# Reordering the first microseconds of a GeGLU feed-forward kernel: x's first rows by token halves, gate rows first on ScalarE's queue

## The chip, the cores and the metric

The kernel runs on one core of one Trainium2 chip. The metric is the device time of one execution in microseconds (us). The kernel before took 272.92, 274.2 and 273.94 us in three runs, so its median is 273.94 us and the runs are 1.28 us (0.47%) apart from end to end. One more execution was profiled; every line of a profile shown here comes from such a profiled execution, and its times count from the first instruction of the span.

Engine names in the profile: PE is TensorE's matmul, PEld TensorE's weight load, DVE is VectorE, ACT is ScalarE, POOL is GpSimd, SP is SyncE. SPq and ACTq are the instruction streams of SP and ACT when they issue DMAs (transfers).

## The reference

```python
B, S, D, F = 32, 32, 1024, 3584          # x is 1024 tokens by 1024, all bf16
def reference(x, w_gate, w_up, w_down):
    return (gelu_tanh(x @ w_gate) * (x @ w_up)) @ w_down
```

Two products of 1024 x 1024 by 1024 x 3584, an elementwise GELU and product, and one product back of 1024 x 3584 by 3584 x 1024.

## The kernel before

**Tiling.** Both stages are done on quadrants, by a scheme that needs seven products of half-sized quadrants in place of eight (Strassen's, in the form with few additions). The 1024 tokens are two blocks of `NB` = 512, the inner dimension D is two halves of 512. A half is `KD` = 4 slices of 128 (128 is `P`, the number of partitions). In the code `b11`, `b12`, `b21`, `b22` are the four quadrants of x transposed (inner dimension on partitions, tokens along the row): first index the half of D, second index the token block. `b21`, the one that matters here, is the second half of D for the first 512 tokens, as four slices `k` of 128 x 512. The gate weight's quadrants are called a11 and a12 (first and second half of D), the up weight's a21 and a22.

**The first stage** walks the 28 feature tiles of 128 columns in 14 chunks of two. For the first `NAHEAD` = 24 tiles one of the products, a12 times `b21`, is done before everything else, in six groups of `KB` = 4 tiles (`a12_ahead[0]` to `a12_ahead[5]`, each 128 x 4 x 512 of `w_gate`), and parked in SBUF in the tiles `ahead`. This is what PE does in the first 26 us or so, and the change lies wholly in how that work starts. The second stage (lines 407 to 590) is the product with `w_down`; the change does not touch it.

**How b21 comes in.** x lies in memory with tokens as rows, and PE wants the inner dimension on partitions. Slices 2 and 3 of `b21`, and the other three quadrants, come by transposing DMAs (`load_xT`, line 216). For slices 0 and 1 (`KQ` = 2) that is done on PE: `load_nat` (line 196) brings x's rows as they are into `x_nat`, PE transposes them in pieces of 128 x 128 against an identity matrix (line 264), and VectorE copies the result from the PSUM tile `tp` into `b21` (line 267). One call `transposed(dt)` does one slice: two halves of 256 tokens, two pieces each, a copy after each half.

**Order of work.** The whole kernel is under a manual schedule: each engine executes its instructions in the order in which the code issues them, and an instruction that waits holds everything behind it on its engine. Nothing is reordered by a planner. So the order around the change is:

- SP's queue: `x_nat` for slice 0 (all 512 tokens, 128 KB), then slices 0 and 1 of `a12_ahead[0]` one by one (128 KB each), the transposing DMA for slices 2 and 3 of `b21`, and then the rest of `a12_ahead`, the first weights and the other quadrants of x.
- ScalarE's queue: `probe`, a read of a few bytes of `w_gate` into a tile that nothing reads; `x_nat` for slice 1 (128 KB); slices 0 and 1 of `a12_ahead[1]` (256 KB); then its compute instructions, of which the first is a GELU that loads the function table.
- PE: `NWARM` = 6 matmuls of ones into `warm_ps`, whose result nobody reads; the four transposes of slice 0; then the loop of lines 327 to 332. It goes over slice `k` and token half, with four half products (128 x 256, one for each tile `j` of `a12_ahead[0]`) in each of its four rounds. After the first round come the four transposes of slice 1. Then eight products with `a12_ahead[1]` (slices 0 and 1), and so on through the groups.
- VectorE: the four copies out of `tp`, then its half of the copies to `ahead`.

What PE waits for here: the first transpose for `x_nat`; a half product for its slice of `a12_ahead[0]` and for VectorE's copy of its half of `b21`.

Of the kernel before, what the change touches and what calls it, by code (L numbers as in the profile page):

```python
# [13 lines left out]
def kernel(  # L14
# [20 lines left out]
    nc = tc.nc  # L35
    P = nc.NUM_PARTITIONS
    fp32 = mybir.dt.float32
    f32r = mybir.dt.float32r
    bf16 = mybir.dt.bfloat16
# [10 lines left out]
    KD = DT // 2  # L50
# [4 lines left out]
    KQ = DT // 4  # L55
    HF = FT // 2
    MT = NB // P
    NWARM = 6
    KB = 4
    QF = HF // 2  # L60
    batches = [(0, KB), (KB, QF), (QF, QF + KB), (QF + KB, HF)]
# [2 lines left out]
    wg_r = w_gate.rearrange("(dt dp) f -> dp dt f", dp=P)  # L64
# [8 lines left out]
    xpool = one.enter_context(tc.tile_pool(name="x", bufs=1))  # L73
# [33 lines left out]
    def acc(tag):  # L107
        return ps1.tile([P, NB], fp32, name=f"ps{tag}", tag=tag, bufs=BANKS[tag])
# [5 lines left out]
    b21 = xpool.tile([P, KD, NB], bf16, name="b21")  # L114
# [72 lines left out]
    ones_w = nc.const_aps.tensor(1.0, [P, P], bf16)  # L187
    ones_m = nc.const_aps.tensor(1.0, [P, NB], bf16)
    ident = xpool.tile([P, P], bf16, name="ident")
    make_identity(nc, ident)  # L190
    NB_P = NB // P
    HALF = NB_P // 2
    x_nat = spool.tile([P, NB_P, KQ * P], bf16, name="x_nat", tag="s1")

    with tc.manual_schedule():
        def load_nat(eng, dt, p0, p1):
            eng.dma_start(  # L197
                out=x_nat[:, p0:p1, dt * P : (dt + 1) * P],
                in_=xf[p0 * P : p1 * P, (KD + dt) * P : (KD + dt + 1) * P].rearrange("(b p) d -> p b d", p=P),
            )  # L200

        assert KQ == 2
        load_nat(nc.sync, 0, 0, NB_P)


        probe = xpool.tile([P // 8, KQ, 2], bf16, name="probe")
        nc.scalar.dma_start(out=probe, in_=wg_r[::8, KD : KD + KQ, :2])

        def load_ahead(i, k0, k1, eng=nc.sync):
            f0 = i * KB  # L210
            eng.dma_start(
                out=a12_ahead[i][:, k0:k1, :],
                in_=wg_r[:, KD + k0 : KD + k1, f0 * P : (f0 + KB) * P],
            )

        def load_xT(nb, d0, d1):
            t = ((b11, b12), (b21, b22))[d0 // KD][nb]
            nc.sync.dma_start_transpose(
                out=t[:, d0 % KD : (d1 - 1) % KD + 1, :], in_=xf[nb * NB : (nb + 1) * NB, d0 * P : d1 * P]
            )  # L220

        load_ahead(0, 0, 1)
        load_nat(nc.scalar, 1, 0, NB_P)
        load_ahead(0, 1, 2)
        load_xT(0, KD + KQ, DT)
        load_ahead(1, 0, KQ, nc.scalar)
        a12_ahead += [spool.tile([P, KD, KB * P], bf16, name="a12b", tag=t) for t in ("s2", "s4", "s1", "s3")]
        for i in (0, 1):
            load_ahead(i, KQ, KD)
# [24 lines left out]
        warm_ps = acc("A")  # L254
        for _ in range(NWARM):
            nc.tensor.matmul(warm_ps, lhsT=ones_w, rhs=ones_m, start=True, stop=True)

        tps = [[ps1.tile([P, HALF * P], bf16, name="tp", tag="A", bufs=BANKS["A"]) for _ in range(2)] for _ in range(KQ)]

        def transposed(dt):  # L260
            for half, tp in enumerate(tps[dt]):
                p0 = half * HALF
                for b in range(HALF):
                    nc.tensor.transpose(  # L264
                        tp[:, b * P : (b + 1) * P], x_nat[:, p0 + b, dt * P : (dt + 1) * P], ident
                    )
                nc.vector.tensor_copy(b21[:, dt, p0 * P : (p0 + HALF) * P], tp)

        transposed(0)

        def prod(ps, lhs, rhs, start):
            for k in range(KD):
# [9 lines left out]
        def product_ahead(ps, i, j, k0=0, k1=KD, cols=slice(None)):  # L282
            for k in range(k0, k1):
                nc.tensor.matmul(  # L284
                    ps[:, cols],
                    lhsT=a12_ahead[i][:, k, j * P : (j + 1) * P],
                    rhs=b21[:, k, cols],
                    start=(k == 0 and not cols.start),
                    stop=(k == KD - 1),
                    skip_group_check=True,  # L290
                )
# [35 lines left out]
        for k in range(KQ):  # L327
            for half in range(2):
                for j in range(KB):
                    product_ahead(ps[0][j], 0, j, k, k + 1, slice(half * HALF * P, (half + 1) * HALF * P))  # L330
                if k == half == 0:
                    transposed(1)
        for j in range(KB):
            product_ahead(ps[1][j], 1, j, 0, KQ)
        for i in (0, 1):
# [283 lines left out]
```

## Time and profile before

| | |
|---|---|
| three runs | 272.92, 274.2, 273.94 us |
| span of the profiled execution | 272.0 us |
| time of that execution around its span | not shown; the three runs are 0.9 to 2.2 us above the span |
| PE busy in the span | 267.1 us (98%) |
| VectorE, POOL, ScalarE busy | 74%, 44%, 43% |
| PE's first matmul | 0.78 us |
| first transpose | 3.30 us |
| first half product | 4.31 us |
| first matmul with slice 1 of `a12_ahead[0]` | 6.28 us |

The page's first parts give busy times and a row of 40 slices; its chain of waits names what the end of the span hangs on. Times of single instructions come from the timeline, which merges neighbours of one kind: a line gives the start, the length of the merged piece, the instruction and, in brackets, how long the engine stood idle before it and what released it. A matmul's length there includes the time until its result is out, so successive matmuls overlap; their pace is read from the distance of their starts.

### The profile page before, as it was taken

To read this page: it belongs to the slowest core of one execution; us is meant where nothing else is said; L and a number is where in the kernel's file an instruction comes from. 1 tells how busy PE (TensorE), PEld (TensorE's weight loads), DVE (VectorE), ACT (ScalarE), POOL (GpSimd) and SP (SyncE) were. 2 spreads that over 40 slices of the span, in tenths; PEclk is the share of its full clock that TensorE was granted. 3 is DMA by queue.
4 is the path that set the end of the run, shared out by engine and by line. 5 is a ranking of instruction groups with operands and counts; after the bars stand their busy time and mean duration, and the time that the engine had idled before them with its cause. 6 is when DMAs were issued, how large, how long until landed. Compare 5 with 4: busy or idle time off the path is not lost.

```text
span 272.0 us, 3399 instructions
## 1 busy us (share of the span) xinstructions
PE 267.1 (98%) x1199; PEld 193.4 (71%) x1212; DVE 201.2 (74%) x205; ACT 116.1 (43%) x189; POOL 119.3 (44%) x60
## 2 busy tenths in 40 slices
PE   8999999999999999999999999999999999999995
PEld 4444776886787688688688687764458888888884
DVE  1448998886976876876787458569999999997721
ACT  2335865545644643645636535434000307770000
POOL 1090099976995994994995978000000000000000
PEclk9999999999999999999999999999999999999999
DMA  7999130504505505415234290005981437855111
GB/s 174 323 227 281 39 99 17 158 25 130 154 2 154 154 4 154 128 27 157 69 88 118 50 319 17 0 2 182 356 273 60 158 112 253 276 187 174 54 61 58
DMA packets 56048, 35.86 MB, mean 132 GB/s; under 512 B 9824, under 2 KB 56032, under 8 KB 56032
## 3 DMA queue, kind: packets, MB, share of 16 engines
q1 hardware_dynamic: 52736, 33.17, 42.6%
q10 hardware_dynamic: 3296, 2.49, 2.9%
q8 instruction: 9, 0.15, 0.2%
q14 instruction: 7, 0.06, 0.1%
HBM read 31.72 MB, written 2.10 MB: 124 GB/s over the span
## 4 chain that ended last, share of the span: by engine, by line
PE 97%; DMA 1%; issue 0%; SPq 0%; DVE 0%
PE psA L273 38%; PE psA L425 24%; PE psC L273 19%; PE psC L425 7%; PE psA L284 5%; PE psC L284 3%; PE psC L588 1%; DMA a12a<-in_w_gate_dram 1%; SPq L197 0%; PE tp L264 0%; DVE o_last L589 0%
## 5 line engine op out<-in xcount | busy, mean ns | idle before, releaser
L273 PE MATMUL psA<-t,s 128*128 128x512 f32 x224 | 57.2, 397 | 0.0
L248 ACT ACTIVATE h<-c 128x512 bf16<-128x512 f32 x56 | 34.6, 631 | 41.6 <-DVE c L303 41.6
L273 PEld LDWEIGHTS psA<-t,s 128*128 128x128 f32 x224 | 42.1, 188 | 9.5
L170 POOL TENSOR_TENSOR s<-wu 128x1024 fp32r<-128x1024 bf16 x13 | 28.8, 2215 | 32.9 <-DMA wu<-in_w_up_dram 27.9
L171 POOL TENSOR_TENSOR s<-s,wg 128x1024 fp32r<-128x1024 f32 x14 | 31.7, 2263 | 15.0 <-DVE s L170 14.0
L173 POOL TENSOR_TENSOR s<-wg,wu 128x1024 fp32r<-128x1024 bf16 x13 | 28.4, 2188 | 0.0
L273 PE MATMUL psA<-b,wg 128*128 128x512 bf16 x119 | 27.8, 379 | 0.6
L273 PE MATMUL psA<-t,a22r 128*128 128x512 f32 x112 | 27.9, 391 | 0.0
L273 PE MATMUL psC<-t,s 128*128 128x512 f32 x112 | 27.9, 391 | 0.0
L273 PE MATMUL psC<-b22r,s 128*128 128x512 f32 x112 | 27.6, 389 | 0.0
L303 DVE TENSOR_TENSOR c<-sn,psA 128x512 f32<-128x512 f32 x32 | 21.8, 682 | 6.7 <-PE psA L273 5.7
L308 ACT COPY sn<-psC 128x512 f32<-128x512 f32 x28 | 16.4, 590 | 20.9 <-PE psC L273 15.2
L273 PEld LDWEIGHTS psC<-t,s 128*128 128x128 f32 x112 | 21.0, 188 | 4.5
L273 PEld LDWEIGHTS psA<-t,a22r 128*128 128x128 f32 x112 | 21.0, 188 | 4.5
L273 PEld LDWEIGHTS psC<-b22r,s 128*128 128x128 f32 x112 | 21.0, 188 | 4.4
L303 DVE TENSOR_TENSOR c<-sn,psC 128x512 f32<-128x512 f32 x28 | 19.2, 688 | 6.5 <-PE psC L273 6.5
L273 PEld LDWEIGHTS <-wg 128*128 128x128 bf16 x128 | 11.8, 98 | 15.3 <-issue 2.4
L172 POOL TENSOR_TENSOR s<-wg,s 128x1024 fp32r<-128x1024 bf16 x10 | 21.6, 2158 | 0.8
L402 DVE TENSOR_TENSOR lo<-c,h 128x512 bf16<-128x512 f32 x14 | 20.4, 1459 | 0.9
L308 ACT COPY sn<-psA 128x512 f32<-128x512 f32 x32 | 18.4, 592 | 6.1 <-PE psA L273 6.0
L303 DVE TENSOR_TENSOR c<-ahead,psA 128x512 f32<-128x512 f32 x24 | 16.4, 687 | 4.0 <-PE psA L273 2.4
L321 DVE TENSOR_TENSOR hi<-h,psA 128x512 bf16<-128x512 bf16 x14 | 9.6, 688 | 12.4 <-PE psA L273 12.4
(85 smaller groups left out, 381.0 us busy)
## 6 DMA issues: line engine op xcount, KB each, us to landing
wu<-in_w_up_dram SPq DMA_DIRECT2D x14, 512.0 KB, 4.0
wdb<-in_w_down_dram SPq DMA_DIRECT2D x12, 512.0 KB, 4.9
wg<-in_w_gate_dram SPq DMA_DIRECT2D x9, 512.0 KB, 5.2
wdb<-in_w_down_dram SPq DMA_DIRECT2D x12, 384.0 KB, 4.5
v<-in_w_down_dram SPq DMA_DIRECT2D x4, 512.0 KB, 6.4
out_dram<-o_sb ACTq DMA_DIRECT2D x15, 128.0 KB, 1.7
wg<-in_w_gate_dram SPq DMA_DIRECT2D x6, 256.0 KB, 4.6
v<-in_w_down_dram SPq DMA_DIRECT2D x4, 384.0 KB, 7.5
```

The lines of the kernel that those rows point to most:

```text
L170: yield engs[0].tensor_tensor(s1, a21, a22, ADD)
L171: yield engs[1].tensor_tensor(s2, s1, a11, SUB)
L172: yield engs[2].tensor_tensor(s4, a12, s2, SUB)
L173: yield engs[3].tensor_tensor(s3, a11, a21, SUB)
L248: nc.scalar.activation(h, src, ACT.Gelu_apprx_tanh)
L273: nc.tensor.matmul(ps, lhsT=lhs[:, k, :], rhs=rhs[:, k, :], start=(start and k == 0), stop=(k == KD - 1), skip_group_check=True,)
L284: nc.tensor.matmul(ps[:, cols], lhsT=a12_ahead[i][:, k, j * P : (j + 1) * P], rhs=b21[:, k, cols], start=(k == 0 and not cols.start), stop ...
L303: tt(t, s, ps, ADD)
L308: nc.scalar.copy(t, ps)
L321: tt(g_of(ft)[:, :NB], h0, psa, MUL)
L402: tt(g_of(ft)[:, NB:], added(sn5[fl], psa[fl]), h1[fl], MUL)
L425: nc.tensor.matmul(banks[m], lhsT=lhs(k)[:, m * P : (m + 1) * P], rhs=rhs(k), start=(start and k == 0), stop=(k == HF - 1), skip_group_che ...
```

## The change

It has four pieces, all in the head of the program.

1. `x_nat` for slice 0 comes in two transfers of 256 tokens (64 KB each), and slice 1 (128 KB) third, all three on SP's queue.
2. The `probe` read is gone. ScalarE's queue now begins with the two slices of `a12_ahead[0]` (128 KB each), followed by the 256 KB of `a12_ahead[1]` as before. SP's queue has lost the two slices of `a12_ahead[0]`, and its transposing DMA is the fourth transfer as it was before.
3. PE's warm-up is five matmuls of 128x512 in place of six. `transposed` now does one half of one slice. Only slice 0's first half (two transposes, one copy) stands ahead of the loop, followed by `NFILL` = 6 matmuls of 128x128 of ones into `warm_ps`.
4. After the first round of four half products come the other six transposes in a row: slice 0's second half, slice 1's first, slice 1's second; and VectorE's three copies after them.

Everything behind the loop is as before; PE's instructions are the old ones less one warm-up matmul, and six fillers more.

```diff
-    NWARM = 6
+    NWARM = 5
+    NFILL = 6
...
-        load_nat(nc.sync, 0, 0, NB_P)
-
-
-        probe = xpool.tile([P // 8, KQ, 2], bf16, name="probe")
-        nc.scalar.dma_start(out=probe, in_=wg_r[::8, KD : KD + KQ, :2])
+        load_nat(nc.sync, 0, 0, HALF)
+        load_nat(nc.sync, 0, HALF, NB_P)
+        load_nat(nc.sync, 1, 0, NB_P)
...
-        load_ahead(0, 0, 1)
-        load_nat(nc.scalar, 1, 0, NB_P)
-        load_ahead(0, 1, 2)
+        for k in range(KQ):
+            load_ahead(0, k, k + 1, nc.scalar)
+        load_ahead(1, 0, KQ, nc.scalar)
         load_xT(0, KD + KQ, DT)
-        load_ahead(1, 0, KQ, nc.scalar)
...
-        def transposed(dt):
-            for half, tp in enumerate(tps[dt]):
-                p0 = half * HALF
-                for b in range(HALF):
-                    nc.tensor.transpose(
-                        tp[:, b * P : (b + 1) * P], x_nat[:, p0 + b, dt * P : (dt + 1) * P], ident
-                    )
-                nc.vector.tensor_copy(b21[:, dt, p0 * P : (p0 + HALF) * P], tp)
-
-        transposed(0)
+        def transposed(dt, half):
+            p0, tp = half * HALF, tps[dt][half]
+            for b in range(HALF):
+                nc.tensor.transpose(tp[:, b * P : (b + 1) * P], x_nat[:, p0 + b, dt * P : (dt + 1) * P], ident)
+            nc.vector.tensor_copy(b21[:, dt, p0 * P : (p0 + HALF) * P], tp)
+
+        transposed(0, 0)
+        for _ in range(NFILL):
+            nc.tensor.matmul(warm_ps[:, :P], lhsT=ones_w, rhs=ones_w, start=True, stop=True)
...
                 if k == half == 0:
-                    transposed(1)
+                    for dt, h in ((0, 1), (1, 0), (1, 1)):
+                        transposed(dt, h)
```

## The prediction

> **What bounds the kernel now.** I read the page's busy times and chain first, to see whether a few tenths won in the head reach the end.
>
> ```profile
> PE 267.1 (98%) x1199; PEld 193.4 (71%) x1212; DVE 201.2 (74%) x205; ACT 116.1 (43%) x189; POOL 119.3 (44%) x60
> ...
> PE 97%; DMA 1%; issue 0%; SPq 0%; DVE 0%
> ```
>
> PE is busy for 98% of the span and the chain that ended last is 97% PE. So behind the head the kernel is one row of matmuls, and what the head gains or loses arrives at the end in full, unless PE then meets a transfer. The chain of the first 8 us, in order of time (start, length, what), shows what is not PE:
>
> ```profile
> 0.74 0.45 SPq L197
> 1.19 0.06 issue
> 1.25 3.02 DMA a12a<-in_w_gate_dram
> 4.26 0.05 issue
> 4.31 0.61 PE psC L284 x2
> ```
>
> SP issues `x_nat`, then the first gate slice; that lands at 4.27, and from 4.31 the chain is PE. The timeline of the head shows what PE did meanwhile:
>
> ```profile
> 0.78 2.72 PE L256 MATMUL psA<-const-bfloat16-1.0 128*128 128x512 bf16 x6 [0.78 <-PEq L603]
> 3.30 0.62 PE L264 MATMUL tp<-ident,x_nat 128*128 128x128 bf16 x4
> 3.75 0.51 DVE L267 COPY b<-tp 128x256 bf16<-128x256 bf16 x2 [3.75 <-PE tp L264]
> 4.31 0.61 PE L284 MATMUL psC<-b,a12a 128*128 128x256 bf16 x2 [0.39 <-DMA a12a<-in_w_gate_dram]
> 5.14 0.63 PE L264 MATMUL tp<-ident,x_nat 128*128 128x128 bf16 x4
> 5.57 0.53 PE L284 MATMUL psC<-b,a12a 128*128 128x256 bf16 x2
> 5.93 0.38 PE L284 MATMUL psA<-b,a12a 128*128 128x256 bf16 x2
> 6.28 1.64 PEld L284 LDWEIGHTS <-a12a 128*128 128x128 bf16 x13 [0.25 <-DMA a12a<-in_w_gate_dram]
> ```
>
> Paces, from distances of starts: up to 5.6 us a transpose costs 0.107 us (four from 5.14 to 5.57) and a 128x256 half product 0.21 (four from 4.31 to 5.14); from 5.93 a half product costs 0.11. The warm-up matmuls stand 0.43 apart, later 128x512 ones 0.216. So PE runs at half pace until about 5.85 us, although the page's clock row shows 9 throughout. Idle on PE: 0.39 us for the first gate slice, and about 0.13 before 6.28 for the second. Landings and the sharing of the DMA engines (bytes per issue, us to landing; then the two queues' share of the engines' time from 3.3 to 3.6 us, q1 being SP's and q10 ScalarE's):
>
> ```profile
> x_nat<-in_x_dram SPq DMA_DIRECT2D x1, 128.0 KB, 2.5
> x_nat<-in_x_dram ACTq DMA_DIRECT2D x1, 128.0 KB, 3.2
> a12a<-in_w_gate_dram SPq DMA_DIRECT2D x2, 128.0 KB, 3.7
> ...
> q1 hardware_dynamic: 59, 0.05, 49.2%
> q10 hardware_dynamic: 114, 0.03, 49.1%
> ```
>
> ```profile
> 2.20:2.70 0.50, 0.50 (x3) 0.15 (x1) 0.00 (x0) 0.41 (x1) 0.00 (x0) 1.00 1.12 245
> 2.70:3.30 0.60, 0.60 (x2) 0.00 (x1) 0.00 (x0) 0.60 (x1) 0.00 (x0) 1.00 1.13 233
> 3.30:3.80 0.50, 0.50 (x5) 0.35 (x4) 0.06 (x1) 0.48 (x2) 0.00 (x0) 1.00 1.10 249
> ```
>
> In the second fence the last two numbers of a line are the share of the 16 engines' time and GB/s. From 2.2 us the engines are full, and two busy queues get half of them each. So the order of the queues, not the time of issue, decides what lands when.
>
> **The change part by part.** The profiled execution shows only its span, 272.0 us; the median is 1.9 above that. I work out the change on the head's times and add it to the median.
>
> *Rows and gate slices.* Before, `x_nat` for slice 0 had the engines nearly alone (96.6% of their time from 2.2 to 2.7 went to SP's queue) and landed at 0.74 + 2.5 = 3.24. Now its first half has half the bytes, but ScalarE's queue carries the first gate slice beside it from the start. Half the bytes at half the engines' time is the same landing, 3.24, so the first transpose starts at about 3.30, as before. Bounds: not before PE is through five warm-ups, 0.78 + 5 x 0.43 = 2.91; and not after 0.74 + 3.2 = 3.94, if it took as long as the shared 128 KB of the ScalarE row. I take 3.30, since the balance of bytes and share gives it. The first gate slice, issued at 0.73 in place of 1.25, lands at 0.73 + 3.0 = 3.7; the second, issued about 1.2, lands near 1.2 + 3.0 = 4.2 in place of 6.2. Slice 1's rows are now third on SP's queue, issued near 1.64: everything on both queues ahead of them is what was ahead of the old one, plus up to 256 KB of gate rows at their side. Bounds: 1.64 + 3.2 = 4.8 and, if they land with the last of the same 768 KB, which had landed by 1.73 + 4.6 = 6.3, then 6.3. I take 5.0, close to the lower, since ScalarE's queue gets half the engines, not all.
>
> *PE, one warm-up fewer, six fillers.* The warm-up ended before the rows anyway, so nothing is won by it. Two transposes and six 128x128 fillers at 0.107 make 0.86, so the first half product is free at 3.30 + 0.86 = 4.16. Its other condition: the second transpose starts at 3.41, its result takes the 0.31 of the row before (four starts from 3.30, the copy at 3.75 after the second), the copy 0.29, together 4.09. The fillers decide by 0.07. Start 4.16 against 4.31: -0.15.
>
> *Transposes moved behind the first round.* First round 4.16 + 4 x 0.21 = 5.01; slice 0's second half to 5.22, its rows long there; slice 1's four to 5.65. Before, these two transposes stood in the wait ahead of 4.31, where they cost nothing; now 2 x 0.107 = +0.21 stand on the path. The second round needs the copy of slice 0's second half: 5.12 + 0.31 + 0.04 + 0.29 + 0.05 = 5.81, so PE waits 0.16. Before, that copy was done at 4.26: a new wait. VectorE has nothing else queued; its copies to `ahead` start at 9.96. Round two then needs 0.11 x 4, a little of it before the pace doubles at 5.85: it ends at 6.27. The third round finds its gate slice there (0.13 won) and its copy done (5.81 + 0.29 = 6.10, cover 0.17). It starts at 6.27 against 6.28.
>
> *Queues passed and the rest.* Both queues issue three transfers at about 0.45 to 0.5 us each, as before, so SP's transposing DMA leaves near 2.2 in place of 2.32 and ScalarE's table load at about 2.3 again. Slices 2 and 3 of `b21` land at 2.32 + 4.9 = 7.2 and the next of `a12_ahead[0]` at 3.71 + 4.2 = 7.9; PE wants both near 8.9, so even 0.9 us earlier meets no wait. The probe's few bytes cost only 0.45 us of issue on ScalarE; that first gate rows may come slower without it is inside the upper bound.
>
> *Sum:* -0.15 + 0.21 + 0.16 - 0.13, less 0.10 since part of round two now runs at the doubled pace: -0.01 us. With the bounds: rows at 2.91 give 6.06 at the third round (-0.2), rows at 3.94 give 6.81 (+0.5).
>
> [...] The rows put the doubling at 5.85 us, 5.1 after PE's first matmul; my sum leaves it there. [...]
>
> **Rivals.** *A, the stream really starts earlier.* If the pace doubles by about 4 us in most runs, the old kernel still waits until 6.28 for its second gate slice, while the new one is held only by slice 1's rows: at 4.8, four transposes at half their cost (0.22), the second round at 5.0 and the third at 5.4. That is -0.9: 273.0; with the runs' scatter it can fall below 272.6. For it: the 0.25 wait at 6.28. Against: in the profile PE is slow until 5.85, which hides most of that wait.
>
> *B, the change doesn't bring x earlier but later.* Slice 1's rows land at 6.3, behind all gate rows. Then transposes to 6.6, round two to 7.0, round three at 7.0: +0.7, 274.6. For it: full engines and 512 KB of gate rows on the other queue. Against: the even split at 3.3 to 3.6.
>
> *C, slower: the doubling comes late.* Five warm-ups end at 2.91 and PE then waits for rows, so the work that leads up to the doubling is broken earlier. If it counts anew from 3.30, it comes at 3.30 + 5.1 = 8.4, and 2.5 us at half pace cost 1.3; if from round two at 5.81, 10.9, costing 2.5. Middle 1.9: 275.8. It decides if a pause near 0.4 us restarts it. Against: the old 0.39 pause ended at 4.31 and the doubling still came 1.5 later. For: a pause up to 1.0 if the rows land at 3.94.
>
> **How the numbers follow.** Forecast 0.58, A 0.20, B 0.10, C 0.12. Half a per cent, about what a measurement can tell from no change here, is 1.37 us: 272.57 to 275.31. Faster: nearly half of A, 0.09, and 0.01 of the forecast by scatter. Slower: 0.11 of C and 0.02 of B. The rest, 0.77, is within. I forecast 273.9. The range goes down to 272.6 (A with 0.4 of scatter, leaving out 0.09) and up to 275.2 (B with scatter and C's cheap end, leaving out 0.11).
>
> **What would show it.** Right: first transpose near 3.3, first half product near 4.2 released by fillers or the copy, a new PE wait of 0.1 to 0.2 on VectorE before round two, no wait for the second gate slice, round three near 6.3. A transpose waiting on `x_nat` past 5.3 speaks for B; half products still 0.21 apart after 6.5 for C; spacing of 0.11 before 4.5 for A.

## The result: slower, by a late transfer and a late doubling of PE's pace

The changed kernel takes 275.89 us (median of 8 runs, 274.7 to 276.98) against 273.99 us for the kernel before beside it: 1.0075 times, 95% interval 1.0053 to 1.0097. Its runs fall into two groups, four at 274.70 to 275.27 and four at 276.51 to 276.98, 1.5 us apart. The execution whose trace follows took 276.53 us, so it is one of the upper group; its span is 274.7 us.

First the page: busy times, and the chain that ended last by engine.

```profile
PE 269.9 (98%) x1217; PEld 194.6 (71%) x1217; DVE 200.0 (73%) x205; ACT 116.0 (42%) x189; POOL 119.3 (43%) x60
...
PE 97%; DMA 2%; SPq 0%; DVE 0%; issue 0%
```

Still a row of matmuls; but DMA's share of the chain is 2% in place of 1%. Where it is, the chain of the head tells (start, length, what):

```profile
0.74 0.44 SPq L198
1.18 0.06 issue
1.24 0.47 SPq L198
1.71 0.05 issue
1.76 4.43 DMA x_nat<-in_x_dram
6.19 0.05 issue
6.24 0.61 PE tp L261 x4
```

The three issues of x's rows stand on SP's queue one after the other, and the third, slice 1's 128 KB, takes 4.43 us to land: 6.19. Before, the same rows left from ScalarE's queue at 1.21 and landed 3.2 us later. The timeline shows what PE does meanwhile:

```profile
0.77 2.29 PE L254 MATMUL psA<-const-bfloat16-1.0 128*128 128x512 bf16 x5 [0.77 <-PEq L601]
...
3.35 0.40 PE L261 MATMUL tp<-ident,x_nat 128*128 128x128 bf16 x2 [0.29 <-DMA x_nat<-in_x_dram]
...
4.18 0.64 PE L281 MATMUL psC<-b,a12a 128*128 128x256 bf16 x2
...
5.04 0.42 PE L261 MATMUL tp<-ident,x_nat 128*128 128x128 bf16 x2
...
6.24 0.61 PE L261 MATMUL tp<-ident,x_nat 128*128 128x128 bf16 x4 [0.78 <-DMA x_nat<-in_x_dram]
...
7.49 0.63 PE L281 MATMUL psC<-b,a12a 128*128 128x256 bf16 x2
```

Up to 5.04 all is as forecast. Then PE stands before slice 1's transposes: the bracket counts 0.78 us of idle, from the end of the modelled tail of the transposes before; by the pace, PE had no work from 5.25 to 6.24, a full microsecond. The third round (first use of the second gate slice) starts at 7.49 against 6.28: 1.21 us lost. The spans differ by 2.7 us, so as much again is lost later, and it isn't in a wait. Groups of matmuls by shape from 7.5 to 10.4 us (count, busy us, mean ns of one), the changed kernel first, the kernel before second:

```profile
L281 PE MATMUL psA<-b,a12a 128*128 128x256 bf16 x5 | 1.7, 417 | 0.0
L281 PE MATMUL psA<-b,a12a 128*128 128x512 bf16 x3 | 1.5, 631 | 0.0
```

```profile
L284 PE MATMUL psA<-b,a12a 128*128 128x512 bf16 x11 | 2.7, 379 | 0.0
L284 PE MATMUL psC<-b,a12a 128*128 128x512 bf16 x4 | 1.0, 379 | 0.0
```

A 128x512 matmul takes 631 ns here, 379 before: at 10.4 us PE still runs at half pace. Its starts stand 0.427 apart up to 10.48, then one of 0.273, then 0.217, which puts the doubling at about 10.6 us, against 5.86 in the trace of before. From 7.49 to 10.6 half the time is lost, 1.55 us by this estimate. Together 1.21 + 1.55 = 2.76, the 2.7 between the spans. The lower group of runs lies 1.1 above the old median, which would be the price of the pause alone; the upper one, by this trace, has the late doubling too. No trace shows a run of the lower group.

Two questions follow. What makes slice 1's rows late? And is it the pause that makes the doubling late?

### The profile page after: what moved, and what is told of

Read it like the earlier page. It is cut to its first block, busy times and chain, and to the rows that moved or that the text cites. A ratio compares the mean times of both kernels' runs of the same rounds, so it can differ in the third digit from the quotient of the medians.

```text
span 274.7 us, 3423 instructions
## 1 busy us (share of the span) xinstructions
PE 269.9 (98%) x1217; PEld 194.6 (71%) x1217; DVE 200.0 (73%) x205; ACT 116.0 (42%) x189; POOL 119.3 (43%) x60
## 3 DMA queue, kind: packets, MB, share of 16 engines
q10 hardware_dynamic: 3008, 2.62, 3.0%
## 4 chain that ended last, share of the span: by engine, by line
PE 97%; DMA 2%; SPq 0%; DVE 0%; issue 0%
PE psA L270 38%; PE psA L423 24%; PE psC L270 18%; PE psC L423 7%; PE psA L281 5%; PE psC L281 3%; DMA x_nat<-in_x_dram 2%; PE psC L586 1%; SPq L198 0%; PE tp L261 0%; DVE o_last L587 0%
## 5 line engine op out<-in xcount | busy, mean ns | idle before, releaser
L270 PE MATMUL psA<-b,wg 128*128 128x512 bf16 x128 | 29.4, 380 | 0.0
```

The costliest lines, as they stand in the source:

```text
L270: nc.tensor.matmul(ps, lhsT=lhs[:, k, :], rhs=rhs[:, k, :], start=(start and k == 0), stop=(k == KD - 1), skip_group_check=True,)
```

## The experiments

Eight more kernels were measured, each against the kernel before on the same chip: 273.74 us (24 runs) beside the new transfers alone, the new PE order alone, the filled pause and slice 1's rows on ScalarE's queue; 273.69 us (35 runs) beside the other four. None of them leaves out any of the work. The ratios are the estimates on record and differ from the quotients of the medians by up to 0.1%.

| kernel | median us | to before, 95% interval | runs from, to |
|---|---|---|---|
| changed kernel | 275.89 | 1.0075 (1.0053 to 1.0097) | 274.70, 276.98 |
| new transfers alone | 276.27 | 1.0094 (1.0057 to 1.0131) | 275.70, 278.00 |
| new PE order alone | 274.19 | 1.0025 (1.0001 to 1.0050) | 273.40, 276.25 |
| new PE order alone, six warm-ups | 273.72 | 0.9993 (0.9972 to 1.0013) | 273.23, 274.11 |
| changed, pause filled | 274.74 | 1.0032 (1.0016 to 1.0049) | 274.32, 275.15 |
| changed, slice 1's rows on ScalarE's queue | 276.06 | 1.0077 (1.0049 to 1.0104) | 274.60, 276.29 |
| changed, transposing DMA later | 275.94 | 1.0077 (1.0049 to 1.0104) | 274.55, 277.95 |
| changed, 256 KB of gate rows later | 274.98 | 1.0042 (1.0023 to 1.0062) | 274.51, 275.63 |
| before, transposing DMA later, fillers | 273.55 | 0.9989 (0.9964 to 1.0013) | 272.84, 274.61 |

### The two halves of the change

New transfers, old order on PE (the edits to `load_nat`, `probe` and `load_ahead` alone):

> The old order of PE with the new order of transfers. If the pause comes from where slice 1's rows stand among the transfers (theory Q): those rows land near 6.2 us again, PE pauses about 0.8 us ahead of slice 1's transposes, and the time is 275.0 to 276.0. If it comes from the new order on PE (theory P): no pause over 0.4 us and 273.7 to 274.4.

New order on PE, old transfers:

> The new order of PE (five warm-ups, fillers, six transposes behind the first round) with the old transfers. Theory Q: slice 1's rows land near 4.4 us as before, no pause over 0.4 us, and the time is 273.6 to 274.4. Theory P: 275.3 or more.

The transfers alone cost more than the whole change: 276.27. Slice 1's rows land at 6.56 (issued at 1.76, 4.8 us), and PE, counted by pace, is idle for some 1.3 us before their transposes, of which the bracket shows 1.13:

```profile
6.61 0.61 PE L261 MATMUL tp<-ident,x_nat 128*128 128x128 bf16 x4 [1.13 <-DMA x_nat<-in_x_dram]
```

The time is a little above the range of theory Q and the pause longer than the 0.8 expected, but the side is clear. The order on PE alone gives 274.19, inside theory Q's range, so the loss lies in the transfers. But 0.25% is, just, above nothing (the interval starts at 0.01%), and four of its twelve runs stand at 274.88 to 276.25; that tail is taken up below. Its waits on PE and PEld from 2 to 7 us (what waited, on what, us in all, times, longest):

```profile
PEld L264 <- DMA x_nat<-in_x_dram: 1.2, 1, 1.2
...
PEld L284 <- DMA a12a<-in_w_gate_dram: 0.2, 1, 0.2
PE psC L284 <- DVE b L265: 0.2, 1, 0.2
```

There is the new wait on VectorE's copy, 0.16 us by the timeline. The 0.2 on `a12a` is for the first gate slice, at 4.38; the second is not waited for.

### What makes the rows late

Back on ScalarE's queue, between the two gate slices:

```diff
-        load_nat(nc.sync, 1, 0, NB_P)
...
-        for k in range(KQ):
-            load_ahead(0, k, k + 1, nc.scalar)
+        load_ahead(0, 0, 1, nc.scalar)
+        load_nat(nc.scalar, 1, 0, NB_P)
+        load_ahead(0, 1, 2, nc.scalar)
```

> The changed kernel with slice 1's rows on ScalarE's queue between the two gate slices, in place of third on SP's queue. Theory Q: they land by 1.2 + 3.2 = 4.4 us, the second gate slice near 5, no pause over 0.4 us before slice 1's transposes, and the time is 273.5 to 274.4. If the rows are late wherever they stand, because the engines are full until 6 us: they land after 5.3 and the time is 275 or more.

Its landings (KB each, us to landing), of the two 64 KB transfers the second alone:

```profile
x_nat<-in_x_dram ACTq DMA_DIRECT2D x1, 128.0 KB, 2.9
```

```profile
x_nat<-in_x_dram SPq DMA_DIRECT2D x1, 64.0 KB, 4.1
```

Slice 1's rows do land at 1.21 + 2.9 = 4.1. But the time stays at 276.06. The second half of slice 0's rows now stands last ahead of SP's transposing DMA and takes 4.1 us where the changed kernel needs 2.6; and the 256 KB for `a12_ahead[1]` take 7.0 us, so that PE, at full pace by then, stands idle for 1.5 us at 9.32. The wait went to other transfers. This suggested the transposing DMA as the culprit, so it was moved one place back:

```diff
+        load_ahead(0, KQ, KD)
         load_xT(0, KD + KQ, DT)
...
-        for i in (0, 1):
-            load_ahead(i, KQ, KD)
+        load_ahead(1, KQ, KD)
```

> The changed kernel with SP's transposing DMA moved one place back, behind 256 KB of gate rows. If the transposing DMA directly behind slice 1's rows holds up their last pieces (theory X): they land before 5.6 us in place of 6.2, the pause on PE is under 0.5 us, the doubling comes near 6 in most runs and the median is 274.0 to 275.0. If it is ScalarE's 512 KB of gate rows beside them (theory Y): landing still 5.9 to 6.3 and 275.4 to 276.3.

Theory X falls: the rows take 5.0 us and land at 6.7, later than before the edit and beyond theory Y's 5.9 to 6.3 too; 275.94. Last, the 256 KB of gate rows were taken from ScalarE's queue (`a12a_ahead[1]` in the text on record is `a12_ahead[1]`):

```diff
-        load_ahead(1, 0, KQ, nc.scalar)
         load_xT(0, KD + KQ, DT)
+        load_ahead(1, 0, KQ)
```

> The changed kernel with the 256 KB of a12a_ahead[1] taken off ScalarE's queue and put on SP's behind the transposing DMA; ScalarE's queue then carries only the first two gate slices beside x's rows. Theory Y: slice 1's rows land before 5.4 us, no pause over 0.3 us there; the 256 KB land later, near 8, and PE may wait up to 1 us for them ahead of its first product with that tile. Theory X: rows still land at 5.8 or later. Time by Y 274.0 to 275.3, by X 275.5 or more.

Theory Y's numbers come out here, although the transposing DMA again stands directly behind slice 1's rows. The timeline of this kernel has slice 1's transposes in one row with slice 0's second half:

```profile
5.05 0.85 PE L261 MATMUL tp<-ident,x_nat 128*128 128x128 bf16 x6
```

and the queues' shares of the engines' time from 3.3 to 4.3 us (packets, MB, share; q1 SP's, q10 ScalarE's) show what changed, the changed kernel first, this one second:

```profile
q10 hardware_dynamic: 156, 0.16, 65.9%
q1 hardware_dynamic: 163, 0.04, 17.7%
```

```profile
q1 hardware_dynamic: 477, 0.12, 52.6%
q10 hardware_dynamic: 31, 0.02, 5.9%
```

In this microsecond SP's queue, with the rows on it, got 17.7% of the engines' time while ScalarE's gate rows got 65.9%; with the 256 KB gone, 52.6%, and the rows land at 1.74 + 3.5 = 5.2. The price is paid behind: the 256 KB arrive at 7.82 and PE waits for them. The chain:

```profile
3.64 4.18 DMA a12a<-in_w_gate_dram
7.82 0.05 issue
7.87 1.25 PE psA L281 x5
```

So 274.98, 1.29 above the kernel before. Counted by pace, PE is idle for 0.67 us before 7.87, and that is nearly all of the 0.7 by which the two spans differ (272.7 and 272.0); the rest of the 1.29 is not accounted for. Why SP's queue got less than half isn't settled. It is not that the engines were full: the two shares add up to 83.6% in the changed kernel and 58.5% here. In the changed kernel the two queues moved nearly as many packets, 156 on ScalarE's and 163 on SP's, and by the MB beside them SP's were a quarter as large; from 2.2 to 2.7 us the counts were 102 and 210.

### The pause and the doubling

The changed kernel with its pause filled:

```diff
-                    for dt, h in ((0, 1), (1, 0), (1, 1)):
-                        transposed(dt, h)
+                    transposed(0, 1)
+                    for _ in range(10):
+                        nc.tensor.matmul(warm_ps[:, :P], lhsT=ones_w, rhs=ones_w, start=True, stop=True)
+                    for h in range(2):
+                        transposed(1, h)
```

> The changed kernel with ten more fillers of 128x128 (10 x 0.107 = 1.07 us) between slice 0's second half and slice 1's transposes, where PE stood idle for 1.05 us. If that idle stretch is what delays the doubling of PE's pace (theory G): the doubling comes near 6 us in all runs, the runs gather at 274.5 to 275.3 in place of two groups 1.5 us apart, median near 275.0. If the late doubling has another cause, such as one warm-up fewer: 275.7 to 276.2 and still two groups.

Ten matmuls whose result nobody reads make the kernel faster: 274.74, all twelve runs within 0.83 us, no upper group. The transposes of slice 1 still start only at 6.45, so the late rows cost what they did; what has gone is the late doubling, which the trace now has at 6.40. Matmuls from 7.5 to 10.4 us, in this kernel:

```profile
L281 PE MATMUL psA<-b,a12a 128*128 128x512 bf16 x8 | 1.9, 379 | 0.0
```

What does the clock do around a pause? The trace records when the granted clock changes, and one kernel, the one with the transposing DMA moved, shows three changes in its head, at 4.10, 7.51 and 10.92 us: full, half, full. The stretches of that kernel between the three changes (length, PE's busy us and matmuls, ... , clock, DMA share, GB/s):

```profile
4.10:7.51 3.41, 1.50 (x18) 1.23 (x17) 0.71 (x3) 0.00 (x0) 0.00 (x0) 1.00 1.14 214
7.51:10.92 3.41, 3.41 (x14) 1.83 (x13) 0.07 (x1) 0.00 (x0) 0.00 (x0) 0.50 1.12 330
```

In the first PE was busy for 1.50 of 3.41 us, because it waited 1.91 us for slice 1's rows; for the whole next stretch it was granted half the clock, although it never stopped. Beside it stand PE's busy times over the same length ahead of the doubling in other traces: 3.02 ahead of 5.86 in the kernel before, 2.96 ahead of 6.40 with the pause filled, 3.03 ahead of 9.64 with the new transfers alone, and 2.62 in the 3.39 us ahead of 3.39 in the last kernel of the table. With the new transfers alone PE was busy for 2.14 of the 3.41 us from 2.82 to 6.23, and the pace was still half behind them.

The trace of the changed kernel has no record of the clock. From 3.8 to 7.2 us, the stretch that holds the pause, the profile counts 2.62 us of 3.40 as busy, the modelled tails of the matmuls among them, and the pace stayed at half until about 10.6. That is as much as the 2.62 us ahead of 3.39 that were followed by the full clock. So the busy time alone doesn't tell the cases apart, and what the clock goes by is not shown.

Nor is it shown that the pause is alone in making the doubling late here: by the pace, PE also stood idle for some 0.45 us behind the five warm-ups (0.77 + 5 x 0.427 = 2.91, to 3.35). What the experiments show is that the pause decides: filled, the late doubling is gone with five warm-ups, and with the new transfers alone it is there (9.64) with six.

Last, the tail of the runs with the new PE order alone. The same kernel with six warm-ups:

> The new order of PE with the old transfers, but six warm-ups in place of five, so that the stretch before the first transpose is filled. If the idle 0.5 us after five warm-ups makes the doubling late in some runs (theory G): at most one run in ten stands 1 us above the lowest group, and the median is 273.6 to 274.0. If the new order itself costs it: 274.1 to 274.5 with a third of the runs high, as with five.

```profile
PEld L264 <- DMA x_nat<-in_x_dram: 0.6, 1, 0.6
```

273.72, and no run of twelve above 274.11. The wait of the weight load for x's rows, 1.2 us with five warm-ups, is 0.6. The two were measured beside nearly equal times of before, and their medians are 0.47 us apart; but their intervals overlap, and four high runs of twelve against none is few. That the sixth warm-up is worth 0.47 us is thus likely, not shown. So is the reason, fewer late doublings: the trace with five warm-ups is of a run from the lower group, in which the pace doubles at about 4.4 (by the distance of starts), and no trace shows a high run.

And a kernel built from before, meant to beat both:

```diff
         transposed(0)
+        for _ in range(4):
+            nc.tensor.matmul(warm_ps[:, :P], lhsT=ones_w, rhs=ones_w, start=True, stop=True)
```

with the transposing DMA one place back as above.

> The kernel before with two edits: its transposing DMA one place back behind 256 KB of gate rows, and four fillers of 128x128 (0.43 us) in the 0.39 us in which PE waited for the first gate slice. If the transposing DMA holds up what stands ahead of it (theory X), the second gate slice lands before 5.8 in place of 6.2, PE does not wait for it, and with the stream unbroken the late doublings go: 273.0 to 273.6, runs closer together. By theory Y the second gate slice lands at 6.0 to 6.3 and the time is 273.5 to 274.0.

Its second gate slice is no longer waited for (the third round starts at 5.38), and its profiled execution, with the doubling at 3.39, took 272.92. But the median is 273.55 and the interval, 0.9964 to 1.0013, holds 1. As both edits were made at once and theory X fell above, what ended the wait isn't told apart. No version here is shown to beat the kernel before.

Not measured: the removal of `probe` alone, five warm-ups in the old order, the changed kernel with six warm-ups (which would tell what the gap behind five adds to the pause), and the new PE order with six warm-ups and the transposing DMA one place back. The first gate slice, read without the probe, landed 2.4 us after its issue in place of 3.0, which gives no sign that its removal hurt.

## Why the prediction was wrong

**What held.** The head does reach the end in full: 1.21 + 1.55 of the head against 2.7 of the span. The first transpose started at 3.35 (forecast 3.30), the first half product at 4.18, set by the fillers (4.16). The landing of slice 0's first half was right too, but by luck: the balance of half the bytes at half the engines isn't what happened. From 1.7 to 2.2 us SP's queue had 2.1% of the engines' time and ScalarE's 52.7; from 2.2 to 3.3 it had 46 to 48 against some 60. The new wait on VectorE ahead of the second round is 0.16 in the kernels where nothing hides it (0.16). The second gate slice is not waited for.

**Step that failed first: "Slice 1's rows ... I take 5.0".** They landed at 6.19, near the upper bound of 6.3, which I had worked out and set aside because "ScalarE's queue gets half the engines, not all". That share was read from 0.3 us of the trace of before, and for other transfers. The same trace has ScalarE's queue at 73.0% against 36.6 from 3.3 to 3.8 us and at 69.8 against 23.2 from 3.8 to 4.3, so the even split was an instant, not a rule. In the changed kernel, in the microsecond that counted, it was 65.9% to 17.7%. Moving the 256 KB away brings the landing to 5.2 and ends the pause. Rival B had the mechanism and the place, but too small a price (0.7 against 1.2): it reckoned with the doubled pace that the same pause prevented.

**Step that failed second: "my sum leaves it there", the doubling at 5.85.** It came at about 10.6 in the trace, which is of the upper half of the runs. The pause that the first step missed stands ahead of it; with that pause filled, the doubling came at 6.40 and the upper group was gone. Rival C had the price nearly right (1.3 to 2.5 against 1.55); that its middle, 275.8, lies beside 275.89 is luck, since the median here falls between two groups and C has no late rows in it. Its cause was at most a part of it: it blamed the 0.4 us behind the warm-ups, and asked whether the count starts anew. Nothing here shows a count that starts anew. The 0.5 us behind the warm-ups did not keep the pace of the new PE order alone from doubling at about 4.4 in its trace; what they add to the pause of rival B in the changed kernel is not shown. I had given B and C 0.10 and 0.12 as alternatives; they were one case, whose sum, some 1.1 to 1.2 in all runs and some 1.5 more in half of them, is the 1.9 measured. The 3.41 us at half the clock in the kernel with the transposing DMA moved cost half of that by estimate, 1.7 us, which is near the 1.5 us between the two groups; the prediction's sum has no such price in it.

**A term costed at nothing: "One warm-up fewer ... nothing is won by it".** True of the rows' time, but it left something out: with five, PE idles for 0.5 us before the first transpose. The two kernels with the new PE order differ by 0.47 us in the median, which is likely but not clear of the noise.

## What to carry to other kernels

At the head of a kernel, ask of a pause of PE not only how long it is, but what it does to the moment when the pace doubles: here a pause of a microsecond cost 1.21 us by itself and, in the traced run, 1.55 more at half pace behind it. That moment isn't known beforehand (the first doubling stands anywhere from 3.39 to 10.6 us in these traces), and the runs of one kernel can fall into two groups, here 1.5 us apart. Where a transfer may come late, put idle matmuls ahead of the instruction that waits for it: ten of them brought this kernel from 275.89 to 274.74 us. When transfers are regrouped over queues, the one to look at is the last on each queue whose data PE needs early; give it the late end of its bounds unless what shares the engines with it has been measured for those very transfers.

## What was not expected of the hardware

- In the kernel with the transposing DMA moved PE had the full clock from 4.10 us, paused for 1.91 us, and was granted half the clock from 7.51 to 10.92 us, although it no longer stopped.
- The changed kernel ran at half pace until 10.6 us, but its trace has no record of the clock, its page no row of clock tenths, and the mean given for it is 1.000. Only the distance of matmul starts shows the half pace.
- Ten matmuls whose result nobody reads narrowed the runs from 2.28 us apart to 0.83 and took 0.9 us off the kernel's distance to the one before (1.90 to 1.00).
- In one microsecond of the changed kernel SP's queue, with transfers under way, got 17.7% of the engines' time beside 65.9% for ScalarE's, while the engines were not full (83.6% together).
